# Last frequency group of tile 0 by sixteen combined matrices instead of through DRAM; two neighbouring pieces of work moved

## The chip, the cores and the metric

One core of one Trainium2 chip. The metric is the device time of one execution in microseconds. The kernel before took 700.67 us, the median of 3 runs (699.94 to 701.03).

## The reference

An adaLN block over 2048 tokens of width 512, batch 1. `mod = silu(c) @ w_mod` gives six rows of shifts, scales and gates.

```
h = layernorm(x) * (1 + ca) + sa
x = x + ga * S4(h)        # per channel: causal convolution of length 2048 by FFT, plus h * Dskip
h = layernorm(x) * (1 + cb) + sb
x = x + gb * (mish(h @ w1 + b1) @ w2)      # 512 -> 1792 -> 512
```

The convolution's kernel K(l) = Re sum_n C_n exp(dt A_n l) dt B_n has 128 complex terms per channel.

## The kernel before

**Convolution.** The 512 channels are four blocks b of 128. The transform over the 2048 tokens is done in two steps by matmuls, of length 32 and of length 64, with 32 frequencies r in the first. A block's frequencies go through in eight groups of four; v = 8b + s counts groups, so 24 to 31 belong to the last block. For a group, `s_ubu` (L575) and `s_ubk` (L591) take the input and the convolution's kernel through the step of length 64 with the matrices `mf` (128 x 32 x 128, group s reads slices 4s to 4s + 3), `s_ug` copies the first on ACT, `s_prod` (L597) multiplies the two spectra in four DVE operations, `s_t1` (L611) transposes the product on TensorE and copies it on ACT to `yt`, and `s_invb` (L618) applies the inverse of length 64 (`mi`), copies the result on ACT to `z`, and stores `z`, 256 KB, to DRAM (`zd`).

The inverse of length 32 sums over all 32 frequencies of a block, which lie on different partitions of what is needed, so it reads `zd` back as `zt`. Blocks 0 to 2 do it in `s_inva` with `inva_mm` (L669, one call for two token tiles, K = 64 matmuls with 32 columns of weights). A token tile j, 0 to 3, is 512 tokens. `inva_add` (L678) adds the result to x on DVE and stores x to DRAM (`x2d`).

**The last stage** is `drain` (L932), an order written out by hand. A loop over the last block's groups, i = 0 to 7, runs `s_prod`, a split of w1 (`w1_split`, L822: a rounded high part on ACT, the rest on DVE), the transforms for later groups, `s_t1` and `s_invb`. For the last block `zt3` is one tile of 128 partitions x 2 halves x 2048: `zt_rows(s)` (L952) loads group s, 32 rows of 8 KB, onto every fourth partition of half s // 4. `inva_half(h, js)` (L955) does the inverse of length 32 over one half, K = 128, for the token tiles js; PSUM adds the halves up. The loads of groups 0 to 4 are issued on SP at i = 3 to 7, behind that iteration's store of `z`; those of 5 and 6 on POOL; that of 7 on SP, and all later DMAs of certain kinds are pinned behind it (`pin["SP"]`).

Behind the loop: statistics of the layernorm for blocks 0 and 1, `inva_mm` for block 2 (two calls) with its adds, the first half of block 3 for all four token tiles, its second half for tile 0, `inva_add(b, 0)` and tile 0's statistics, the second half of tiles 1 to 3, `gate_row` (L489, four matmuls and ACT's copy `gbb`), then layernorm of tile 0: `ln_scales` (a row of small DVE operations), `ln_qs` (`xn`, two on DVE, two on ACT), `ln_tq` (transposes into `pln`), `ln_h` (`hh`, the MLP's input split in two).

**MLP.** Tile 0 goes through `mm1_plain(f)` for f = 0 to 13 with `load_w2(0, f)` (w2 is multiplied by the gate and split); `mm2(0, f - 2)` follows f by two. Tiles 1 to 3 run on a scheme with seven products. The splits of w1 number 5 to 7 and more serve f of 7 and up.

**Order.** TensorE, ACT and DVE run in the order of the program in `drain` and for f = 0 and 1 (`InOrder`, L123). SP's and POOL's order is chosen by the framework's planner, with program order as priority; tiles of a pool share buffers: `z` has three, `w1s`, `w2s` share three (tag `ws`), most PSUM results share six banks (tag `pb`).

Of the kernel before, what the change touches and what calls it, by code (L numbers as in the profile page):

```python
# [18 lines left out]
P = 128  # L19
# [33 lines left out]
def _constants():  # L53
    r = np.arange(32)
    s = np.arange(64)
    j = np.arange(64)
    i = np.arange(32)
    th = 2 * np.pi * ((j[None, :, None] * (4 * r[:, None, None] + 1 + 128 * s[None, None, :])) % 8192) / 8192.0
    mf = np.zeros((32, 2, 64, 2, 64))
    mf[:, 0, :, 0, :] = np.cos(th)  # L60
    mf[:, 1, :, 0, :] = np.sin(th)
    mf[:, 0, :, 1, :] = -np.sin(th)
    mf[:, 1, :, 1, :] = np.cos(th)
    mf = mf.reshape(32, P, P)
    psi = 2 * np.pi * ((i[:, None] * (4 * r[None, :] + 1)) % 128) / 128.0
    da = np.stack([np.cos(psi), -np.sin(psi)], axis=1)
    bdk = np.zeros((4, 32, 2, 4, 32))
    for t in range(4):
        bdk[t, :, :, t, :] = da
    da = da.transpose(0, 2, 1).reshape(32, 64)  # L70
    dj = np.zeros((8, 4, 4, 2, 4, 32))
    for j in range(4):
        dj[:, j, :, :, j, :] = da.T.reshape(2, 4, 8, 32).transpose(2, 1, 0, 3) / 2048.0
    ac = np.zeros((4, 32, 32, 32))
    mc = np.zeros((4, 32, 32, NCO))
    fac = np.concatenate([64 * 8 * np.arange(4), 64 * np.arange(8), 8 * np.arange(8), np.arange(8)])
    for d in range(32):
        ac[0:2, d, d, :] = np.arange(32)
        ac[2:4, d, d, :] = 1
        mc[0:2, d, d, :] = fac  # L80
        mc[2:4, d, d, :4] = 1
    z = np.exp(-2j * np.pi * (4 * np.arange(2048) + 1) / 8192)
    one = ((1 + 1j) / (1 - z)).reshape(64, 8, 4)
    one = np.stack([one.real, one.imag]).transpose(2, 0, 3, 1).reshape(4, 2, 512)
    su = np.zeros((4, 32, 2, 512))
    hl = np.zeros((P, 2))
    for e in range(3):
        m, x = np.frexp(one)
        part = np.ldexp(np.round(m * 256) / 256, x)
        one = one - part  # L90
        for n in range(3):
            su[:, 3 * n + e] = part
            hl[3 * n + e::32, :n] = -1
    f = np.float32
    return {
        "su": su.reshape(P, 1024).astype(f),
        "hl": hl.astype(f),
        "mf": np.ascontiguousarray(mf.transpose(1, 0, 2).reshape(P, 32 * P)).astype(f),
        "mi": np.ascontiguousarray(mf.transpose(2, 0, 1).reshape(P, 32, 2, 4, 4, 4).transpose(0, 1, 2, 4, 3, 5)
                                   .reshape(P, 32 * P)).astype(f),  # L100
        "bdk": np.ascontiguousarray(bdk.transpose(0, 1, 2, 4, 3)).reshape(P, 256).astype(f),
        "bdu": np.tile(da, (4, 1)).astype(f),
        "di": np.tile(da.T / 2048.0, (2, 1)).astype(f),
        "di4": dj.reshape(P, 256).astype(f),
        "ac": ac.reshape(P, 1024).astype(f),
        "mc": mc.reshape(P, 32 * NCO).astype(f),
        "sel": np.tile(np.concatenate([np.eye(32, P, 32 * k) for k in range(4)], axis=1), (4, 1)).astype(f),
        "ident": np.eye(P, dtype=f),
    }
# [9 lines left out]
def s4_block(ctx, tc, io, out):  # L119
    nc = tc.nc  # L120
# [60 lines left out]
    def view(src, offset, ap):  # L181
        return bass.AP(tensor=src.tensor, offset=src.offset + offset, ap=ap)
# [378 lines left out]
    def s_gl(v):  # L561
        b, s = divmod(v, 8)
        GU[v] = cv.tile([P, 512], F32, tag="gu", name=f"gu{v}", bufs=4).rearrange("p (r d) -> p r d", r=4)
        nc.sync.dma_start(GU[v], view(ud, (64 * b + 8 * s) * 64 * P, [[P, P], [P * P, 4], [1, P]]))
# [53 lines left out]
    def s_invb(v):  # L618
        b, s = divmod(v, 8)
        p = bank("pib")  # L620
        for r in range(4):
            T.matmul(p[:, P * r:P * r + P], mi[:, 4 * s + r, :], YT[v][:, r, :], start=True, stop=True)
        z = cv.tile([P, 4, P], F32, tag="us", name=f"z{v}", bufs=3)
        A.copy(z, p.rearrange("p (r d) -> p r d", r=4))
        nc.sync.dma_start(view(zd[b], 8 * s * 64 * P, [[P, P], [P * P, 4], [1, P]]), z)
# [41 lines left out]
    PIA = {}  # L667

    def inva_mm(b, j):  # L669
        for h in range(2):  # L670
            PIA[b, j + h] = bank("pia")
        for a in range(4):
            for h in range(2):
                r = slice(64 * h, 64 * h + 64)
                T.matmul(PIA[b, j + h][32 * a:32 * a + 32, :], di[r, :], ZT[b, j, a // 2 * 2][r, a % 2, :],
                         start=True, stop=True)
# [255 lines left out]
    def drain():  # L932
        b = NB - 1
        bulk[0] = nc.gpsimd
        tables("mish")
        for v in range(v0 + 2, v0 + 5):
            s_gl(v)
        s_kgen(vl)
        s_ks(vl)
        s_t1(v0 - 1)  # L940
        s_ubu(v0 + 1)
        s_ka(vl)
        s_ug(v0 + 1)
        s_tm(vl)
        s_invb(v0 - 1)
        s_ubk(v0)
        mlp_open()
        s_xp(v0 - 1)
        bulk[0] = nc.sync
        zt = big.tile([P, 2, 4, 512], F32, tag="gk", name="zt3")  # L950

        def zt_rows(s, queue):  # L952
            return queue.dma_start(zt[s % 4::4, s // 4], view(zd[b], 8 * s * 64 * P, [[16 * P, 32], [1, 2048]]))

        def inva_half(h, js):  # L955
            for j in js:
                for a in range(4):
                    T.matmul(PIA[b, j][32 * a:32 * a + 32, :], di4[:, h, j, :], zt[:, h, a, :],
                             start=(h == 0), stop=(h == 1), skip_group_check=True)

        def on_pool(f, *a):
            bulk[0] = nc.gpsimd
            f(*a)
            bulk[0] = nc.sync

        for v in range(v0, NG):
            i = v - v0
            s_prod(v)
            if i != 3 and i < 7:
                w1_split(i - i // 4)  # L970
            if i < 3:
                on_pool(w1_load, i + 3)
            if v < vl:
                s_ubk(v + 1)
            if i == 0:
                s_ubu(v + 2)
            s_t1(v)
            if v + 2 <= vl:
                if i:
                    s_ubu(v + 2)  # L980
                s_ug(v + 2)
            if v + 5 <= vl:
                s_gl(v + 5)
            s_invb(v)
            if i in (1, 2):
                s_zl(v0 - 6 + 2 * i)
            if i >= 3:
                zt_rows(i - 3, nc.sync)
        zt_rows(5, nc.gpsimd)
        zt_rows(6, nc.gpsimd)  # L990
        pin["SP"] = zt_rows(7, nc.sync).ins
        ln_stats(0, range(b - 1))
        inva_mm(b - 1, 0)
        inva_add(b - 1, 0)
        inva_mm(b - 1, 2)
        ln_stats(0, (b - 1,))
        for j in range(1, 4):
            inva_add(b - 1, j)
        p = psum.tile([P, 2, 512], F32, tag="pa", name="pia2", bufs=1)
        PIA.update({(b, 0): bank("pia"), (b, 1): bank("pia"), (b, 2): p[:, 0], (b, 3): p[:, 1]})  # L1000
        inva_half(0, range(4))
        inva_half(1, (0,))
        inva_add(b, 0)
        ln_stats(0, (b,))
        inva_half(1, range(1, 4))
        gate_row()
        ln_scales(0)
        xn = cv.tile([P, 4, NB, P], F32, tag="gk", name="xn", bufs=1)
        ln_qs(0, xn)
        for j in range(1, 4):  # L1010
            inva_add(b, j)
        for q in range(4):
            for c in range(NB):
                ln_tq(xn, q, c)
        ln_h()
# [187 lines left out]
    for f in range(FB):  # L1203
        if f == 2:
            pin["V"] = ordered["V"]
            del ordered["V"], ordered["A"]
        if f == FB - 1:
            ln_sums(1)
        mm1_plain(f)
        load_w2(0, f)  # L1210
        if f in (2, 3):
            w1_load(4 + f)
        if f in (4, 5):
            w1_split(2 + f)
        if f in (11, 12):
            ln_at(1, 2 * f - 22)
        if f >= 2:
            mm2(0, f - 2, first=(f == 2))
        if f in (11, 12):
            ln_at(1, 2 * f - 21)  # L1220
        if f >= 2:
            next(todo, None)
        if f == 7:
            ln_load(1)
        if f == 8:
            ln_stats(1, range(2))
        if f == 9:
            ln_stats(1, range(2, NB))
            ln_norm(1)
        if f == 10:  # L1230
            fin_load(0)
# [76 lines left out]
```

## Time and profile before

| what | value |
| --- | --- |
| median of 3 runs | 700.67 us |
| the profiled execution | 699.58 us, span 697.8 us |
| TensorE busy | 628.7 us, 90% of the span |
| DVE, ACT, POOL busy | 496.0, 373.5, 78.5 us |
| mean granted TensorE clock | 0.978 |
| the convolution's last stage, `drain` | ends with `hh`, from 385.19 us |

Times in the profile count from the span's start. PE is TensorE, DVE VectorE, ACT ScalarE, POOL GpSimd, SP the engine that issues most DMAs. An fp32 matmul is two instructions. Names are the program's tiles without their numbers: `pkb` and `pub` are the transforms of kernel and input, `pt` the transpose, `pib` the inverse of length 64, `pia` that of length 32, `pgb` the gate row, `pln` the transposes of the layernorm, `pr` and `pp` the MLP. All compute carries line L131, that of the ordering helper, so the names tell operations apart. A timeline row holds start, length, engine, line, operation, tiles, shape, count, and in brackets the idle time before it with what ended it. A row of the windows holds the stretch, its length, then busy time and count of PE, PEld, DVE, ACT and POOL, the granted clock, the DMA share and GB/s. A row of DMA issues ends with the median us from issue to landing.

### The profile page before, as it was taken

The page shows a single profiled execution, that of the slowest core. Times are in us where ns is not written, and L with a number is a line of the kernel's source. Part 1 is how long each engine was busy: PE and PEld are TensorE (multiplying, and loading weights), DVE is VectorE, ACT ScalarE, POOL GpSimd, SP SyncE. Part 2 cuts the span into 40 slices and gives each one's busy share as a digit, 9 for nine tenths or more (in the row PEclk, how much of TensorE's full clock was granted, in tenths as well). Part 3 has the DMA queues.
Part 4 walks back from the last instruction along what each step waited for, and adds up shares of the span by engine and source line. Part 5 has one row for each costly group of instructions (what it writes and reads, how often), then busy time and mean ns, then how long its engine had stood idle before and what let it go on. Part 6 is the DMA issues. An engine that isn't in the chain of part 4 may idle for free.

```text
span 697.8 us, 15159 instructions
## 1 busy us (share of the span) xinstructions
PE 628.7 (90%) x6077; PEld 512.0 (73%) x6106; DVE 496.0 (71%) x1005; ACT 373.5 (54%) x618; POOL 78.5 (11%) x161
## 2 busy tenths in 40 slices
PE   0566787899999999999987999999999999999997
PEld 0353355677878877888773788888898888998996
DVE  6989986898899988997575799577327733553333
ACT  3465479566886677666561565443436334443231
POOL 1000340060204220000100000000011000010000
PEclk9968989999999999999999999999999999999999
DMA  9928789674328752654687789557334652264232
GB/s 235 220 113 271 182 191 221 190 196 127 77 62 196 196 140 62 167 163 143 181 253 220 233 268 319 183 162 225 112 91 118 193 173 91 92 193 140 91 91 60
DMA packets 107399, 115.89 MB, mean 166 GB/s; under 512 B 12737, under 2 KB 84801, under 8 KB 106433
## 3 DMA queue, kind: packets, MB, share of 16 engines
q1 hardware_dynamic: 93712, 86.34, 43.9%
q0 software_dynamic: 13232, 28.06, 14.4%
q8 instruction: 48, 0.79, 0.5%
q10 hardware_dynamic: 384, 0.52, 0.3%
q14 instruction: 23, 0.18, 0.1%
HBM read 80.28 MB, written 32.51 MB: 162 GB/s over the span
## 4 chain that ended last, share of the span: by engine, by line
PE 71%; DVE 14%; DMA 6%; ACT 5%; issue 2%; SPq 2%; ACTq 0%; DVEq 0%
PE pr L131 29%; PE pp L131 10%; PE pub L131 6%; PE pang L131 6%; PE pkb L131 4%; PE pib L131 4%; PE pkg L131 4%; PE pka L131 4%; DVE ec L131 3%; DVE raw L131 2%; PE pt L131 2%; DMA xt<-x2d 2%; DMA ud<-us 1%; DMA cT<-in_c 1%; DVE bst L131 1%
## 5 line engine op out<-in xcount | busy, mean ns | idle before, releaser
L131 DVE TENSOR_TENSOR ec<-ec,m 128x1024 f32<-128x1024 f32 (+1 forms) x96 | 97.2, 1040 | 13.0 <-ACT ec L131 12.7
L131 ACT ACTIVATE ec<-pang 128x1024 f32<-128x1024 f32 x64 | 65.1, 1034 | 53.9 <-PE pang L131 53.9
L131 PE MATMUL pr<-hh,w 128*128 128x256 f32 (+1 forms) x420 | 78.2, 327 | 0.5 <-ACT hh L131 0.5
L131 PEld LDWEIGHTS pr<-hh,w 128*128 128x128 f32 x420 | 66.5, 188 | 12.7 <-ACT hh L131 1.9
L131 DVE TENSOR_TENSOR mh<-x,pr 128x256 f32<-128x256 f32 x63 | 26.4, 418 | 65.2 <-PE pr L131 64.9
L131 PE MATMUL pp<-w,mah 128*128 128x512 f32 x224 | 70.5, 396 | 0.0
L131 PE MATMUL pr<-w,mah 128*128 128x512 f32 x224 | 70.2, 394 | 0.2 <-DVE w L131 0.2
L131 ACT ACTIVATE mh<-mh,b 128x256 f32<-128x256 f32 x63 | 32.1, 510 | 55.0 <-DVE mh L131 54.7
L131 DVE TENSOR_TENSOR m<-co 128x1024 f32<-128x1024 f32 (+1 forms) x64 | 59.6, 950 | 1.7 <-ACT co L131 1.4
L131 ACT ACTIVATE mh<-pr,b 128x256 f32<-128x256 f32 (+1 forms) x35 | 19.5, 559 | 65.0 <-PE pr L131 65.0
L1033 POOL DMA_DIRECT2D w<-w2d x42 | 22.2, 529 | 282.8 <-PE pp L131 272.1
L131 DVE TENSOR_TENSOR mal<-mh,mah 128x512 fp32r<-128x512 f32 x56 | 38.5, 688 | 21.7 <-ACT mah L131 21.6
L131 PE MATMUL pr<-w,mal 128*128 128x512 f32 x112 | 43.9, 392 | 0.0
L131 PE MATMUL pp<-w,mal 128*128 128x512 f32 x112 | 43.9, 392 | 0.0
L131 PE MATMUL pka<-bdk,ks 128*64 128x128 f32 x512 | 35.9, 284 | 6.9 <-ACT ks L131 6.9
L131 PEld LDWEIGHTS pp<-w,mah 128*128 128x128 f32 x224 | 38.3, 189 | 4.9
L131 DVE TENSOR_TENSOR x<-x,pr 128x256 f32<-128x256 f32 x42 | 17.5, 418 | 33.5 <-PE pr L131 33.5
L131 PE MATMUL pang<-ac,s 128*128 128x256 f32 x128 | 30.0, 318 | 12.2 <-ACT ec L131 12.2
L350 POOL DMA_DIRECT2D s<-pk x48 | 23.8, 504 | 147.9 <-ACT us L131 77.1
L131 PE MATMUL pang<-nac,s 128*128 128x256 f32 x128 | 39.8, 395 | 0.0
L131 PEld LDWEIGHTS pr<-hh,wt 128*128 128x128 f32 x252 | 35.5, 190 | 5.5 <-DVE mh L131 2.2
L131 PEld LDWEIGHTS pkg<-ec 128*32 128x32 f32 x2048 | 33.0, 111 | 8.8 <-ACT us L131 3.2
(153 smaller groups left out, 1351.1 us busy)
## 6 DMA issues: line engine op xcount, KB each, us to landing
w<-w2d POOLq DMA_DIRECT2D x42, 512.0 KB, 3.6
ud<-us SPq DMA_DIRECT2D x64, 128.0 KB, 3.0
gu<-ud SPq DMA_DIRECT2D x32, 256.0 KB, 3.6
zd<-z SPq DMA_DIRECT2D x32, 256.0 KB, 3.6
zt<-zd SPq DMA_DIRECT2D x30, 256.0 KB, 5.1
w2d<-w SPq DMA_DIRECT2D x14, 512.0 KB, 4.1
wm<-in_w_mod SPq DMA_DIRECT2D x24, 256.0 KB, 3.6
xf<-x2d SPq DMA_DIRECT2D x16, 256.0 KB, 4.7
```

The source lines that it names most:

```text
L131: ins = f(*a, **kw)
L350: nc.gpsimd.dma_start(S3[b, i][q, :], pk[32 * i:32 * i + 32, 8 + k, :])
L1033: nc.gpsimd.dma_start(t, w2d[f])
```

## The change

1. For group 31 and token tile 0 alone, the inverses of length 64 and 32 are multiplied together beforehand into sixteen 128 x 128 matrices, `dx` (four frequencies times four tokens of a quad; 1 MB, a new constant). `direct()` applies them to `yt` of group 31 and adds into tile 0's PSUM bank. Tile 0's second half then contracts 96 rows, groups 4 to 6. Group 7's rows are still loaded, for tiles 1 to 3.
2. `dx` is loaded on POOL at i = 3 into slices 0 to 15 of `mf`, whose groups are through by then.
3. `zt_rows(s)` fills 32 neighbouring partitions; the constant `di4` is reordered to match. All eight loads are on SP, each one iteration earlier (group 0 at i = 2); groups 6 and 7 follow the loop.
4. Block 2's two calls of `inva_mm` move from behind the loop to i = 6 and 7, between the transpose and `s_invb`.
5. The first half of tiles 1 to 3 moves behind tile 0's second half.
6. `w1_split(5)` moves from i = 6 into the MLP, behind `load_w2(0, 0)`.

```diff
-    dj = np.zeros((8, 4, 4, 2, 4, 32))
+    dj = np.zeros((4, 8, 4, 2, 4, 32))
     for j in range(4):
-        dj[:, j, :, :, j, :] = da.T.reshape(2, 4, 8, 32).transpose(2, 1, 0, 3) / 2048.0
+        dj[:, :, j, :, j, :] = da.T.reshape(2, 4, 8, 32).transpose(1, 2, 0, 3) / 2048.0
+    dx = np.einsum("rcajq,rci->qrjai", mf.reshape(32, 2, 4, 4, 4, P)[28:, :, :, 0], da.T.reshape(32, 2, 32)[28:] / 2048.0)
...
+        "dx": dx.reshape(P, 16 * P).astype(f),
...
         def zt_rows(s, queue):
-            return queue.dma_start(zt[s % 4::4, s // 4], view(zd[b], 8 * s * 64 * P, [[16 * P, 32], [1, 2048]]))
+            return queue.dma_start(zt[32 * (s % 4):32 * (s % 4) + 32, s // 4], view(zd[b], 8 * s * 64 * P, [[16 * P, 32], [1, 2048]]))
 
-        def inva_half(h, js):
+        def inva_half(h, js, rows=P):
             for j in js:
                 for a in range(4):
-                    T.matmul(PIA[b, j][32 * a:32 * a + 32, :], di4[:, h, j, :], zt[:, h, a, :],
+                    T.matmul(PIA[b, j][32 * a:32 * a + 32, :], di4[:rows, h, j, :], zt[:rows, h, a, :],
                              start=(h == 0), stop=(h == 1), skip_group_check=True)
 
+        def direct():
+            for r in range(4):
+                for j in range(4):
+                    T.matmul(PIA[b, 0][:, P * j:P * j + P], mf[:, 4 * r + j, :], YT[vl][:, r, :], start=False, stop=False,
+                             skip_group_check=True)
...
-            if i != 3 and i < 7:
+            if i != 3 and i < 6:
                 w1_split(i - i // 4)
...
+            if i >= 6:
+                inva_mm(b - 1, 2 * i - 12)
             s_invb(v)
+            if i == 3:
+                nc.gpsimd.dma_start(mf[:, 0:16], io["dx"].rearrange("p (n m) -> p n m", n=16))
             if i in (1, 2):
                 s_zl(v0 - 6 + 2 * i)
-            if i >= 3:
-                zt_rows(i - 3, nc.sync)
-        zt_rows(5, nc.gpsimd)
-        zt_rows(6, nc.gpsimd)
+            if i >= 2:
+                zt_rows(i - 2, nc.sync)
+        zt_rows(6, nc.sync)
         pin["SP"] = zt_rows(7, nc.sync).ins
         ln_stats(0, range(b - 1))
-        inva_mm(b - 1, 0)
         inva_add(b - 1, 0)
-        inva_mm(b - 1, 2)
...
-        inva_half(0, range(4))
-        inva_half(1, (0,))
+        inva_half(0, (0,))
+        direct()
+        inva_half(1, (0,), 96)
         inva_add(b, 0)
         ln_stats(0, (b,))
+        inva_half(0, range(1, 4))
         inva_half(1, range(1, 4))
         gate_row()
...
         load_w2(0, f)
+        if f == 0:
+            w1_split(5)
         if f in (2, 3):
```

## The prediction

> **What bounds the kernel now.** I read the chain that ended last first, from 360 us on, because the change lies between the last frequency groups of the convolution and the first matmul of the MLP. Columns: start, length, what.
>
> ```profile
> 362.20 0.85 ACT w L131
> ...
> 363.07 1.09 DVE w L131
> 364.17 1.27 DVE q L131 x2
> ...
> 365.46 0.77 DVE ug L131 x2
> ...
> 366.36 0.64 PE pt L131 x4
> ...
> 367.08 0.59 ACT yt L131
> ...
> 367.72 2.09 PE pib L131 x8
> ...
> 369.83 0.60 ACT z L131
> ...
> 370.44 2.61 DMA zd<-z
> ...
> 373.07 4.11 DMA zt<-zd
> ...
> 377.32 1.10 PE pia L131 x8
> ...
> 385.19 0.79 ACT hh L131
> ```
>
> The stretch is serial. The sixth split of w1 (ACT then DVE `w`) holds the product of group 31 (`q`, `ug`); the transpose, its copy `yt`, the inverse `pib` and the copy `z` follow; then z goes to DRAM and back, 2.61 + 4.11 = 6.72 us in which tile 0 waits. From `hh` on the chain is mostly TensorE's, so what `hh` gains, the span should gain.
>
> The TensorE timeline shows what can fill the gap:
>
> ```profile
> 361.42 1.06 PE L131 MATMUL pkb<-mf,gk 128*128 128x128 f32 x8
> 362.31 0.60 PE L131 MATMUL pt<-ident,ug 128*128 128x128 f32 x4
> 363.64 1.16 PE L131 MATMUL pib<-yt,mi 128*128 128x128 f32 x8 [0.73 <-ACT yt L131]
> ...
> 369.72 6.07 PE L131 MATMUL pia<-zt,di 64*32 64x512 f32 x64
> 377.32 3.64 PE L131 MATMUL pia<-zt,di 128*32 128x512 f32 x32 [1.52 <-DMA zt<-zd]
> 380.89 1.16 PE L131 MATMUL pgb<-ident,modp 128*128 128x128 f32 x8
> ```
>
> An inverse of eight instructions takes 1.16 us here; the last, at 367.72, took 2.09, because the idle time before it had halved the granted clock (the column before the last two is the clock):
>
> ```profile
> 368.00:370.00 2.00, 2.00 (x16) 1.72 (x24) 0.00 (x0) 0.17 (x1) 0.53 (x1) 0.50 0.33 118
> ```
>
> The row at 369.72 holds block 2's inverse (32 instructions) and the first half of block 3's (32). The second half, 32 instructions for four j's from 377.32 until the gate row starts at 380.89, gives 3.57/4 = 0.89 us for one j of one half.
>
> **The change, part by part.** *The split that leaves i = 6.* The product of group 31 then waits only for `pkb`, which ends at 362.48. With 0.1 of issue it starts near 362.57 instead of 364.17, 1.6 us earlier, and ends 2.06 later (364.17 to 366.23), at 364.63. With the chain's 0.13 and 0.64 the transpose ends at 365.41.
>
> *Block 2's inverse moved into i = 6 and 7.* In the steady loop one such call of 16 instructions stands in this row:
>
> ```profile
> 231.07 1.09 PE L131 MATMUL pia<-zt,di 64*32 64x512 f32 x16
> 232.09 1.16 PE L131 MATMUL pib<-yt,mi 128*128 128x128 f32 x8
> ```
>
> It holds TensorE 1.02 us. The first call goes from 362.75 to 363.77 in the 0.73 us of waiting for `yt`, and delays group 30's inverse from 363.64 to 363.77, 0.13 us. The second follows the transpose, from 365.25 to 366.27, while ACT copies `z` of group 30 and `yt` of group 31 (0.59 each, the second ending near 366.17). Group 31's inverse can start at 366.27. Without the idle stretches ahead of it I price it at 1.16, not 2.09: it ends at 367.43, `z` at 368.05, and the store goes at 368.07 instead of 370.44, 2.37 us earlier. The four results of block 2 now hold banks of PSUM through this; with the six there are I count no wait, and the adds that free them follow the last product on DVE.
>
> *The sixteen direct matrices.* 16 matmuls of 128 columns are 32 instructions; at 0.89 us for eight (`pkb`, 361.42 to 362.31) they cost 3.6 us of TensorE that was not there before. TensorE is free of the inverse at 367.27; one j of the first half takes until 368.16, the sixteen until 371.8. Their weights are one megabyte, loaded through POOL at i = 3, behind this load:
>
> ```profile
> 350.22 0.54 POOL L817 DMA_DIRECT2D w1s<-in_B_w  x1 [4.25 <-DVE q L131]
> ```
>
> ```profile
> w1s<-in_B_w POOLq DMA_DIRECT2D x1, 448.0 KB, 6.2
> ```
>
> ```profile
> mf<-in_mf SPq DMA_DIRECT2D x1, 2048.0 KB, 8.6
> ```
>
> Issued at 350.8, it takes between 8.6/2 = 4.3 us and 6.2 x 1024/448 = 14.2 us: landed by 365.0, before 368.16. For the sixteen I cost it at nothing. But the queues are full there (the last two columns are the DMA share and GB/s):
>
> ```profile
> 355.00:360.00 5.00, 4.74 (x36) 3.83 (x35) 4.12 (x6) 3.58 (x6) 0.00 (x0) 1.00 1.06 312
> 360.00:362.00 2.00, 2.00 (x21) 2.00 (x20) 1.97 (x5) 1.07 (x2) 0.00 (x0) 1.00 0.63 202
> 362.00:364.00 2.00, 1.27 (x12) 1.03 (x11) 1.07 (x2) 1.59 (x3) 0.00 (x0) 1.00 0.44 132
> 364.00:366.00 2.00, 0.80 (x8) 0.61 (x6) 1.97 (x5) 0.59 (x1) 0.52 (x1) 1.00 0.51 139
> ```
>
> One megabyte at 312 GB/s is 3.4 us of backlog, and the idle shares from 360 to 366 add up to 2 x (0.37 + 0.56 + 0.49) = 2.8 us. So it is nearly taken in by 366; for the rest I put 0.2 us on group 6's rows (ends: 0 and 0.6). If it isn't, the stores land late, and `z`, which has three buffers, waits for the store three groups back.
>
> *The row loads.* All eight now issue on SP, behind the stores in program order. Before, group 4's sat behind the last store, at 370.44, with group 7's behind it (the merged row's other one):
>
> ```profile
> 370.90 2.62 SPq L953 DMA_DIRECT2D zt<-zd  x2
> ```
>
> So I place the loads of groups 5 and 6 behind the store at 368.07, 0.46 and some 0.5 us on: 368.5 and 369.0, and with the backlog 369.2. Group 7's waits there for the store's landing, 368.07 + 2.63 = 370.7; block 2's stores of x, pinned behind it, issue some 2.4 us earlier than before and nobody on the path waits for them. Tile 0 now needs group 6's rows last. Landing times of such loads in this stage, first group 6's on POOL, then the one behind the store, at 370.90:
>
> ```profile
> zt<-zd POOLq DMA_DIRECT2D x1, 256.0 KB, 2.9
> ```
>
> ```profile
> zt<-zd SPq DMA_DIRECT2D x1, 256.0 KB, 4.0
> ```
>
> I take 4.0, the row with the same neighbour: landed at 373.2, matmul at 373.3. The quick end is 369.0 + 2.9 = 371.9, and then the sixteen matrices' end and this come together.
>
> *What is late next.* Call the start of the second half's first j t. Before, t = 377.32, and behind it stood three j's (2.7 us), the gate row, ACT's copy `gbb`, ACT's two `xn`. Behind it now stand six j's, since the first half of j = 1 to 3 has moved behind tile 0's.
>
> ```profile
> 382.08 0.59 ACT L131 COPY gbb<-pgb 128x512 f32<-128x512 f32 x1 [11.66 <-PE pgb L131]
> 382.97 1.52 ACT L131 ACTIVATE xn<-xt,nm,rst 128x512 f32<-128x512 f32 x2 [0.30 <-DVE nm L131]
> 385.19 2.79 ACT L131 ACTIVATE hh<-pln,modp 128x512 fp32r<-128x512 f32 x4 [0.70 <-PE pln L131]
> ```
>
> Before, `xn` waited for DVE's `nm`, 382.97 - 377.32 = 5.65 behind t. Now it waits for `gbb`: 7 x 0.893 + 1.16 + 0.03 + 0.59 + 0.02 = 8.05 behind t. So 2.4 us are given back: this is the wait that takes the place of the one removed. With 385.19 - 382.97 = 2.22 more, `hh` starts at t + 10.27, and the change breaks even at t = 374.92. With t = 373.3, `hh` starts at 383.57: **1.6 us earlier**.
>
> *The split moved to f = 0.* It costs 0.85 us of ACT and 1.09 of DVE (the chain's `w`).
>
> ```profile
> 398.61 0.69 DVE L131 TENSOR_TENSOR w<-w2s,w 128x512 fp32r<-128x512 f32 x1
> ...
> 401.13 0.62 PE L131 MATMUL pr<-w,mah 128*128 128x512 f32 x2
> ```
>
> Behind it in order are f = 1's mish, splits and w2: DVE's last of these ends at 399.3, and TensorE asks for it at 401.13, 1.8 us later. The two pieces, 1.94 us in a row, just use that up if nothing of them falls into idle time; I take nothing (ends: 0 and 0.3). The third load of w2 may have to wait for the buffer; its use comes after TensorE's next two matmul groups.
>
> **Sum.** 377.32 - 373.3 = 4.0 us earlier for tile 0's last input, less 2.4 behind it: 1.6 us. The profiled execution took 699.58 (span 697.8), so 698.0 for it; the median of the runs shown is 700.67, 1.1 above it, and from there I predict **699.1 us**. What a measurement of this kernel can tell from no change is about 0.2%, 1.4 us.
>
> **Rivals.** *The sixteen matrices are the bound* (0.16): group 6's rows land within 2.9 us, t = 371.8, `hh` 3.1 us earlier, 697.6. For it: the row of 2.9. Against: that load had no store and no other rows just ahead.
>
> *The new row layout is slow* (0.21). The loads now fill 32 neighbouring partitions instead of every fourth. The first stage loads `xr` in just that shape, 32 partitions by 8 KB, and then `mf` over all 128:
>
> ```profile
> 14.00:18.00 4.00, 0.00 (x0) 0.00 (x0) 3.69 (x13) 1.81 (x3) 0.00 (x0) 1.00 1.04 225
> ...
> 34.00:36.00 2.00, 0.00 (x0) 0.00 (x0) 1.90 (x6) 1.98 (x2) 0.00 (x0) 0.50 1.12 408
> ```
>
> Queues full in both, 225 against 408 GB/s: 256 KB take 1.17 instead of 0.64 us. Groups 5 and 6 behind the store would land 1.0 later, with group 4's tail up to 1.6: t = 374.3 to 374.9, gain 0 to 0.6, 700.4. Against it: part of the `xr` stage is shared with POOL's loads. [...]
>
> *The change doesn't do what it says* (0.09): the 96-row matmuls still wait for group 7's rows, if the order is kept for the whole tile. Then t = 370.7 + 4.11 + 0.14 = 374.9, no gain, 700.6; with slow rows 1.2 us slower. Against it: the 32 instructions of the first half ran before 375.8, while rows of the other half landed until 377.18, so parts of that tile are told apart at least by half.
>
> *Slower* (0.08): the megabyte goes into the half of `mf` that the loop has done with. If the order is kept for `mf` as one, the load waits for the last reader ahead of it, `pub` in i = 3, and the next reader, `pkb` behind the inverse, waits for its landing:
>
> ```profile
> 351.57 1.41 PE pub L131 x9
> 352.98 0.91 PE pib L131 x8
> ```
>
> Issued at 353.0, in 8 us (between the 4.3 and 14.2 above), it lands at 361.0, and `pkb` stands from 353.9 till then: 7.1 us less the 1.6 gained, 5.5 slower, 706.2. It decides as soon as one reader of slices 16 to 31 waits. Against it is again what `zt` shows.
>
> **How the numbers follow.** Forecast 0.46 (t from 372.4 to 374.2, 697.8 to 700.0). Faster: the matrices and the part of the forecast with t under 373.5, for which I put 0.39 of its 0.46: 0.55 together. Same: the rest of the forecast, 0.07, the slow layout and two thirds of the whole-tile wait: 0.34. Slower: the rest of that and `mf`, 0.11. The range goes from the matrices' case, 697.3 with the scatter of the runs, to 701.4, which takes in the slow layout and most of the whole-tile wait; it leaves out about 0.12.
>
> **What would show it.** Right: no `w` between the last two products; the last inverse near 1.2 us at full clock; the last store near 368; `pia` of K = 96 before group 7's rows land; `gbb` ending just ahead of `xn`. If `xn` waits for `nm` instead, the step of 2.4 us is wrong. If `pia` starts over 4.4 us after group 6's issue, the landing is. A PE gap near 401 would be the split; one in `pkb` near 354 the megabyte.

## The result and the profile after

In runs taken side by side the changed kernel took 701.38 us (median of 20) and the kernel before 700.88 (median of 20): a ratio of 1.0007, with a 95% interval of 0.9991 to 1.0023. That is no difference that can be measured: 0.5 us more, between 0.6 less and 1.6 more. The forecast was 1.6 us less.

The profiled execution took 700.8 us, span 699.0, granted clock 0.980. A span alone says little here. Group 30's product starts at 361.20 in this trace and at 360.00 in that of before, but at 184 us, long before anything that was changed, the trace is 1.2 us behind already; over the fourteen executions profiled in this study the product lies anywhere from 359.01 to 363.85. So I compare lengths inside the stage, counted from the start of group 30's product on DVE: to **t**, where TensorE starts block 3's second half for tile 0, and to `hh`, where the MLP starts.

| | before | after | predicted change | measured change |
| --- | --- | --- | --- | --- |
| group 30's product to group 31's | 4.08 us | 2.58 us | -1.6 | -1.50 |
| to the last store's issue | 10.44 | 8.26 | -2.37 | -2.18 |
| to t | 17.32 | 14.32 | -4.0 | -3.00 |
| t to `hh` | 7.87 | 9.93 | +2.40 | +2.06 |
| to `hh` (the stage) | 25.19 | 24.25 | -1.6 | -0.94 |
| `hh` to the end of the span | 312.61 | 313.57 | 0 | +0.96 |

The chain that ended last in the changed kernel, to be read beside that of before (start, length, what):

```profile
367.72 1.10 PE pib L133 x8
...
368.85 0.60 ACT z L133
...
369.46 0.36 SPq L627
...
369.91 0.45 SPq L955
...
370.42 4.96 DMA zt<-zd
...
375.52 6.22 PE pia L133 x56
381.74 1.10 PE pgb L133 x8
...
382.86 0.03 ACT gbb L133
...
383.34 0.82 ACT xn L133
...
385.45 0.79 ACT hh L133
```

The turn through DRAM for group 31, 2.61 + 4.11 us, is gone from the path. In its place stands the load of group 30's rows, 4.96 us, and then a row that was not there: `pia` x56, all of what is left of the four tiles, with the gate row and its copy `gbb` behind it. Before, the chain's `pia` was 8 instructions long and DVE's statistics came next. TensorE's timeline and ACT's say the same; the brackets hold the wait and its end:

```profile
367.65 1.16 PE L133 MATMUL pib<-yt,mi 128*128 128x128 f32 x8
368.74 1.06 PE L133 MATMUL pia<-zt,di 128*32 128x512 f32 x8
369.73 3.84 PE L133 MATMUL pia<-yt,mf 128*128 128x128 f32 x32
375.52 6.22 PE L133 MATMUL pia<-zt,di 96*32 96x512 f32 x56 [1.95 <-DMA zt<-zd]
```

```profile
382.86 0.59 ACT L133 COPY gbb<-pgb 128x512 f32<-128x512 f32 x1 [13.43 <-PE pgb L133]
383.34 1.52 ACT L133 ACTIVATE xn<-xt,nm,rst 128x512 f32<-128x512 f32 x2
```

The sixteen direct matrices (32 instructions) are done 1.95 us before the rows land. `xn` starts 383.34 - 375.52 = 7.82 us behind t with no wait of its own, straight after `gbb`; `nm`, for which it waited before, had ended at 381.15. The queues, in the windows of the changed kernel (the last two columns are the DMA share and GB/s), stay full until 366, where before they had emptied to shares of 0.63, 0.44 and 0.51:

```profile
355.00:360.00 5.00, 4.74 (x40) 4.18 (x39) 3.11 (x5) 3.93 (x6) 0.00 (x0) 1.00 1.03 369
360.00:362.00 2.00, 2.00 (x16) 1.61 (x16) 1.81 (x3) 0.77 (x3) 0.00 (x0) 1.00 1.03 288
362.00:364.00 2.00, 2.00 (x20) 1.88 (x18) 1.52 (x4) 1.25 (x2) 0.00 (x0) 1.00 1.09 358
364.00:366.00 2.00, 2.00 (x26) 1.12 (x24) 1.97 (x5) 0.59 (x1) 0.00 (x0) 1.00 1.08 332
```

### The profile page after: what moved, and what is told of

It is laid out like the page before. It is cut to its first block, busy times and chain, and to the rows that moved or that the text cites. A ratio compares the mean times of both kernels' runs of the same rounds, so it can differ in the third digit from the quotient of the medians.

```text
span 699.0 us, 15258 instructions
## 1 busy us (share of the span) xinstructions
PE 633.9 (91%) x6138; PEld 515.0 (74%) x6138; DVE 496.4 (71%) x1005; ACT 373.8 (53%) x618; POOL 78.3 (11%) x160
## 4 chain that ended last, share of the span: by engine, by line
PE 68%; DVE 15%; DMA 7%; ACT 5%; issue 3%; SPq 1%; ACTq 0%; DVEq 0%
PE pr L133 25%; PE pp L133 9%; PE pub L133 6%; PE pang L133 6%; PE pkb L133 4%; PE pkg L133 4%; PE pib L133 4%; PE pka L133 3%; DVE ec L133 2%; DMA xt<-x2d 2%; DVE raw L133 2%; PE pt L133 2%; PE pia L133 2%; ACT ec L133 2%; DMA wm<-in_w_mod 1%
## 5 line engine op out<-in xcount | busy, mean ns | idle before, releaser
L133 PE MATMUL pang<-rnd,oneb 128*128 128x512 bf16 x128 | 41.9, 410 | 0.0
L352 POOL DMA_DIRECT2D s<-pk x48 | 25.2, 551 | 149.3 <-ACT us L133 77.1
```

Source lines behind the costliest of these rows:

```text
L133: ins = f(*a, **kw)
L352: nc.gpsimd.dma_start(S3[b, i][q, :], pk[32 * i:32 * i + 32, 8 + k, :])
```

## The theories

So 3.0 us were won at t and 2.06 given back behind it. **The order theory**: the first halves of tiles 1 to 3 and the gate row, now queued behind t on TensorE, hold `xn`, and with another order the 2 us come back. **The queue theory**: the megabyte of combined matrices is what makes stores and rows late, and so t. **The layout theory**: it is the rows' 32 neighbouring partitions. Against all three: the direct matrices are worth nothing, and what gain there is comes from the pieces moved. Twelve runs tell them apart. The table has them all; a ratio is to the kernel before on the same chip, t and `hh` are from the profiled execution.

| run | ratio (95% interval) | product of 30 to t | t to `hh` | stage |
| --- | --- | --- | --- | --- |
| before | 1 | 17.32 us | 7.87 | 25.19 |
| changed kernel | 1.0007 (0.9991 to 1.0023) | 14.32 | 9.93 | 24.25 |
| e1, first halves ahead | 0.9963 (0.9942 to 0.9984) | 17.27 | 7.88 | 25.15 |
| e2 and e11, gate row ahead | 0.9959 (0.9939 to 0.9979) | 13.64; 14.14 | 7.88; 7.89 | 21.52; 22.03 |
| e3, before with the new row layout | one run, 701.58 us | 16.47 | 9.05 | 25.52 |
| e4, rows 5 and 6 on POOL | one run, 703.55 us | 14.25 | 11.63 | 25.88 |
| e5, split back | 1.0017 (0.9997 to 1.0037) | 15.83 | 9.93 | 25.77 |
| e6, e1 without the direct matrices | 1.0018 (1.0000 to 1.0036) | 15.75 | 10.19 | 25.94 |
| e7, e1 without the megabyte | 0.9970 (0.9954 to 0.9986) | 14.86 | 7.88 | 22.75 |
| e9, e1 with the megabyte early | 0.9972 (0.9954 to 0.9990) | 14.87 | 7.88 | 22.75 |
| e10, e6 with the old row layout | 1.0003 (0.9980 to 1.0027) | 14.66 | 8.86 | 23.52 |
| e12, e11 with the megabyte early | 0.9967 (0.9945 to 0.9989) | 14.12 | 7.88 | 21.99 |
| e13, e11 with the inverse back | 0.9985 (0.9963 to 1.0006) | 14.85 | 7.89 | 22.74 |

## What holds xn: the order behind t

**e1, all first halves ahead of the direct matrices.**

```diff
-        inva_half(0, (0,))
+        inva_half(0, range(4))
         direct()
...
-        inva_half(0, range(1, 4))
         inva_half(1, range(1, 4))
         gate_row()
```

> The changed kernel with one line's order undone: the first half of all four token tiles stands ahead of the sixteen matrices again. The stage is measured from the start of group 30's product to the start of hh: 25.19 us before (360.00 to 385.19), 24.25 changed (361.20 to 385.45). Theory (the order gives 2.4 us back): three j's at 0.89 us move into TensorE's wait for group 6's rows; its work then ends near 368.74 + 3.57 + 3.84 = 376.1, so t moves from 375.5 to 376.1, but only the gate row and three j's stand behind it, xn waits for nm at t + 5.65 and hh starts at t + 7.87 = 384.0: stage 22.8, 1.5 us shorter than changed. Rival (the order is not what holds xn): the stage gets longer by 0.6, 24.9. In all runs a median of about 699.4 for the theory and 701 for the rival.

Measured: ratio 0.9963 (0.9942 to 0.9984), faster than before. `xn` waits for `nm` again:

```profile
383.26 0.58 ACT L133 COPY gbb<-pgb 128x512 f32<-128x512 f32 x1 [12.85 <-PE pgb L133]
384.17 1.53 ACT L133 ACTIVATE xn<-xt,nm,rst 128x512 f32<-128x512 f32 x2 [0.32 <-DVE nm L133]
```

t to `hh` is 7.88 us, that of before. Its profiled execution shows no gain in the stage for another reason: the stores were late in it, and ACT's copy of `z` for group 30 stood 2.68 us for a store, which put t where it was before. The median of the twelve times is lower all the same; e7 and e9, which have the same instructions from there on, reach t 14.86 us behind the product.

**e2 and e11, the gate's row alone moved ahead.** The first halves of tiles 1 to 3 stay behind t.

```diff
         direct()
+        gate_row()
         inva_half(1, (0,), 96)
...
         inva_half(1, range(1, 4))
-        gate_row()
```

> The changed kernel with the gate's row alone moved ahead of block 3's last half, right behind the direct matrices; the first halves of the other three tiles stay behind it. By the theory that the gate's copy behind the other tiles' halves holds xn, gbb's copy is done before nm, add to hh is 6.75 us as before the change (8.81 in the changed kernel), and the stage 15.4 + 6.75 = 22.2 us where the queues are as in the changed kernel's profile. The rival, that the halves themselves are what is late (PE's order behind t costs the same whatever holds xn), leaves add to hh at 8 us or more.

> The changed kernel with the gate's row alone moved ahead of block 3's last half, as in the single look at it (694.4 us, with 2.2 us of that already there at group 30's product, which scatters from run to run). By the stage alone, 21.52 us from group 30's product to hh against 25.19 before the change, the median is 3.7 us under before: 697.2, ratio 0.9948. If the look was a lucky one and what is late is the landing of the rows, the stage is 23.5 to 25 us as in the changed kernel and the ratio is 0.998 or more. The run with all first halves ahead (ratio 0.9963) lies between.

Measured: one execution of 694.4 us in e2, then over twelve executions in e11 a median of 697.44 against 701.09, ratio 0.9959 (0.9939 to 0.9979). The stages, 21.52 and 22.03 us, say 3.2 to 3.7 us; the median says 3.65, by the ratio 2.9. TensorE and ACT in e11:

```profile
371.08 3.84 PE L133 MATMUL pia<-yt,mf 128*128 128x128 f32 x32
374.75 1.06 PE L133 MATMUL pgb<-ident,modp 128*128 128x128 f32 x8
375.74 6.22 PE L133 MATMUL pia<-zt,di 96*32 96x512 f32 x56
381.98 1.94 PE L133 MATMUL pln<-ident,xn 128*128 128x128 f32 x16
```

```profile
375.84 0.59 ACT L133 COPY gbb<-pgb 128x512 f32<-128x512 f32 x1 [6.02 <-PE pgb L133]
381.41 1.52 ACT L133 ACTIVATE xn<-xt,nm,rst 128x512 f32<-128x512 f32 x2 [4.98 <-DVE nm L133]
```

The same 56 `pia` stand behind t, 6.22 us long, and cost nothing: `xn` waits for DVE's `nm` and starts 5.67 us behind t, and `pln` follows the 56 at once. What cost 2 us was only that eight instructions and a copy, which need nothing of tile 0's sum, were queued last. The order theory holds; the rival in e2's expectation, that the halves themselves are late, falls. e2 and e11 are the same program; in e2 TensorE waited 0.17 us for rows ahead of tile 0's first half, in e11 0.88, and the stages differ by 0.51.

## What makes the rows late

**e3, the kernel before with the new row layout and nothing else** (the constant `di4` reordered, as in the change).

```diff
-            return queue.dma_start(zt[s % 4::4, s // 4], view(zd[b], 8 * s * 64 * P, [[16 * P, 32], [1, 2048]]))
+            return queue.dma_start(zt[32 * (s % 4):32 * (s % 4) + 32, s // 4], view(zd[b], 8 * s * 64 * P, [[16 * P, 32], [1, 2048]]))
```

> The kernel before with one part of the change alone: each row load fills 32 neighbouring partitions, the constant reordered to match; queues and order as before. Landing of the loads before: 2.9 (group 6, POOL), 4.0 (group 4, behind the last store), 4.1 us (group 7). Theory (the layout is slow): each of the last ones lands 0.5 to 1.0 us later, group 7's in 4.6 to 5.1, and the stage grows from 25.19 to 25.7 to 26.2. Rival (the layout is innocent and the changed kernel's 4.96 us is crowding behind the store): 2.9, 4.0 and 4.1 as before, within 0.2, and a stage of 25.2.

Measured: the loads of groups 0 to 3 and 5 take 0.1 to 0.6 us longer (group 5's on POOL 3.45 against 2.98, group 3's 4.23 against 3.67); group 4's takes 5.08 against 3.98, and group 6's 5.22 against 2.87, but it was issued right behind the last store here and ahead of it before. Group 7's, for which tile 0 waits, takes 4.29 against 4.11. The two loads on POOL, as a row of DMA issues in e3:

```profile
zt<-zd POOLq DMA_DIRECT2D x2, 256.0 KB, 4.3
```

Before it was 2.9. The stage is 25.52 us against 25.19, one execution each, and that difference says little of the layout: the last inverse ran at full clock here, 1.16 us in place of 2.09, which takes 0.9 us off, and behind TensorE's wait of 2.14 us the clock was halved (0.50 from 380 to 382), so that t to `hh` took 9.05 in place of 7.87.

**e10 against e6: the layout without the direct matrices.** e6 is e1 without `direct()`, without the load of `dx`, and with all 128 rows in the second half; e10 is e6 with the layout and the constant of before.

```diff
-            if i == 3:
-                nc.gpsimd.dma_start(mf[:, 0:16], io["dx"].rearrange("p (n m) -> p n m", n=16))
...
-        direct()
-        inva_half(1, (0,), 96)
+        inva_half(1, (0,))
```

> The kernel of the run with all first halves ahead, with the sixteen direct matrices and their megabyte left out: block 3 of tile 0 takes all 128 rows of its second half again, so it waits for group 7's rows too; w1's sixth split and block 2's inverse stay where the change put them. This asks what the direct matrices themselves are worth. Theory A (the direct path takes the wait for group 7's rows away): block 3's last half starts when group 7's rows land. Group 31's store is issued 5.2 to 5.3 us behind group 31's product at the earliest with the moved inverse (369.46 - 363.79 = 5.67 in the changed kernel, 370.44 - 363.81 = 6.63 in the run with all first halves ahead), lands 2.6 to 3.5 us later, and the rows take 4.1 to 4.5: from group 30's product to the add 2.58 + 5.67 + 3.0 + 4.3 + 1.1 = about 16.7 with quiet queues, against 15.4 of the changed kernel; since xn waits for nm again (add to hh 6.75), the stage from group 30's product to hh comes to 23.4, and the time to about 698.7, nothing lost against the run with all first halves ahead. Theory B (the megabyte of the direct matrices is what crowds the queues): stores of groups 27 to 30 land in 6.2, 6.6, 4.3 and 2.3 as before the change, not in 8.4 to 11.7, and the stage is shorter than the 25.15 of the run with all first halves ahead by over 1 us. Theory C (the direct path is worth what it says and the megabyte costs nothing): the stores land as late as with it, and the stage is longer by over 1 us.

> The run without the direct matrices, with the rows laid out as before the change (every fourth partition instead of 32 neighbours); nothing else differs from it, and no megabyte is loaded in either. If the row layout is what makes the rows land late, the loads of groups 0 to 2 take 6.7, 4.5 and 3.1 us as before the change, not 10.2, 9.7 and 6.9, group 6's take 2.9 to 4.1 and not 4.5, and the stage falls from 25.94 by 0.5 to 1.5 us. If the rows are late because each load is issued one group earlier, ahead of the store that it waits for, they take 9 us or more in the old layout too, and the stage stays within 0.5 us of 25.9.

The last store and the rows behind it, from the chains of e6 and then of e10:

```profile
370.33 3.86 DMA zd<-z
...
374.21 3.49 DMA zt<-zd
...
377.83 6.47 PE pia L133 x32
```

```profile
368.61 2.35 DMA zd<-z
...
370.98 3.90 DMA zt<-zd
...
375.01 1.97 PE pia L133 x8
```

DMA by DMA, the rows of groups 0 to 2 land in 10.23, 9.72 and 6.91 us in e6 and in 7.63, 7.34 and 5.01 in e10, those of groups 5 and 6 in 4.36 and 4.50 against 3.04 and 3.17. So group 6's load takes about 1.3 us longer in the new layout, and the store beside it too (3.86 against 2.35). These are single executions, but over all ten kernels that issue that load on SP in the new layout it takes 3.90 (e7) to 5.85 us (e1), so e10's 3.17 lies below them all. Of the 2.42 us between the two stages 1.09 lie ahead of t; the rest lies behind it, where e6's clock was halved for longer (0.50 in the windows from 378 to 382, in e10 in the one from 376 to 378). The first three rows are still later in e10 than the 6.71, 4.45 and 3.05 of before, in the same layout; they are issued one group earlier, as the second theory of e10's expectation has it. That this is the reason is argued, since e10 has other pieces of the change as well. Both theories hold in part. The medians do not tell the layouts apart (1.0018 and 1.0003, intervals that overlap). For such a load 4.50 us against 3.17 is 1.4 times as long, where the prediction's two rates, 408 and 225 GB/s, give 1.8; why the layout makes a difference no run shows.

**e7 and e9: the megabyte.** e7 is e1 without the load of `dx`. e9 is e1 with `dx` in a tile of its own, loaded before the loop.

```diff
+        dxt = MW["wt"].tile([P, 16, P], F32, tag="dxt", name="dxt", bufs=1)
+        nc.gpsimd.dma_start(dxt, io["dx"].rearrange("p (n m) -> p n m", n=16))
...
-            if i == 3:
-                nc.gpsimd.dma_start(mf[:, 0:16], io["dx"].rearrange("p (n m) -> p n m", n=16))
```

> The kernel of the run with all first halves ahead without the load of the megabyte of combined matrices: the sixteen matmuls still run, but on what the buffer held from block 2's own matrices, so that the last group of tile 0 is computed wrongly; its time is read for the queues alone. If the megabyte is what delays the stores and rows, those of groups 27 to 29 land in 6.2, 6.6 and 4.3 us as before the change (8.4, 8.8 and 6.5 in the changed kernel, 10.6, 11.7 and 8.7 in the run with all first halves ahead), group 6's rows take 4.0 to 4.4, group 30's store is issued by 5.3 us behind group 31's product, the add of block 3 comes 14.8 to 15.2 us behind group 30's product and hh 21.6 to 22 us: 698.5 to 697.5 by the sums of before. If the row layout or the earlier rows are the cause, the stores land as late as with the megabyte and the stage keeps 24 to 25 us.

> The kernel of the run with all first halves ahead with the combined matrices in a tile of their own, loaded at the start of the drain instead of at its fourth group; the computation is whole. If the megabyte in the middle of the stores is the cost, the landings are those of the kernel without the load (6.2, 6.6, 4.3 for groups 27 to 29, group 6's rows 4.0 to 4.4), the stage from group 30's product to hh takes 21.6 to 22.5 us instead of 25.19 before, and the time is 2.5 to 3.5 us under before: 697.3 to 698.3, ratio about 0.9955. If it is not, the time is that of the run with all first halves ahead, 0.9963, with a stage of 24 to 25 us. If the earlier megabyte delays what else is loaded there (x of the last block, w1), the drain starts later instead, and group 30's product with it, by up to the 2.8 us that a megabyte takes at 370 GB/s.

Measured: the store of group 26 is back at 6.14 us in e7 (8.44 in the changed kernel), but those of 27 and 28 stay at 8.36 and 6.14, and the rows of groups 0 to 2 take 9.03, 8.59 and 6.56 with no megabyte at all. One execution says little: e6, the same program up to there, has 8.43 us for group 26. Over all kernels but before and e3, whose rows are issued later, group 27's store lands in 8.80 to 11.68 us with the megabyte in the middle and in 6.80 to 9.71 without it there (e6, e7, e9, e10, e12), so it does delay the stores beside it. The ratios, 0.9963 with the megabyte in the middle, 0.9970 without it and 0.9972 with it early, do not differ. In e7 and e9 TensorE's own work sets t (7.33 and 7.34 us of it stand between the last inverse and t, with no wait), so neither can show a gain there; e12 below can, and shows none. The queue theory falls: the megabyte delays the DMAs next to it and not the end. (e9's product of group 30 is late, at 363.85 us; in e12, with the same early load, it starts at 359.27, so the load is not what delays it.)

In e7 TensorE runs from the last inverse to the gate row without a wait:

```profile
367.83 1.16 PE L133 MATMUL pib<-yt,mi 128*128 128x128 f32 x8
368.92 3.64 PE L133 MATMUL pia<-zt,di 128*32 128x512 f32 x32
372.49 3.84 PE L133 MATMUL pia<-yt,mf 128*128 128x128 f32 x32
376.25 3.64 PE L133 MATMUL pia<-zt,di 96*32 96x512 f32 x32
```

That is the rival "the sixteen matrices are the bound", made true by e1's order: 7.33 us of work stands ahead of t, and the rows of group 6, landed at 375.58, wait for it.

**e12, both mends at once** (e11 with `dx` in a tile of its own).

> Both mends at once: the gate's row ahead of block 3's last half, and the combined matrices in a tile of their own, loaded at the start of the drain. If the megabyte in the middle of the stores still costs, the stores of groups 26 to 28 land in 7.1 to 8.7 us instead of 9.4 to 9.5, group 6's rows start up to 0.5 us earlier, and the stage is 20.8 to 21.4 us: ratio 0.994. If the megabyte costs nothing once the order is mended, the time is that of the gate's row alone, 0.9948 by its stage. The earlier megabyte may also be paid ahead of the stage: group 30's product at 363.85 in the run with the tile of its own against 359.0 to 361.2 elsewhere; if that is no scatter, the ratio is 0.998 or more with a short stage.

Measured: 0.9967 (0.9945 to 0.9989), stage 21.99 us. The stores do land earlier (8.24, 6.80, 6.07, 3.70 us for groups 26 to 29), and neither the stage nor the median is better than e11's.

**e4, rows of groups 5 and 6 on POOL**, as before the change.

```diff
-            if i >= 2:
+            if 2 <= i < 7:
                 zt_rows(i - 2, nc.sync)
-        zt_rows(6, nc.sync)
+        zt_rows(5, nc.gpsimd)
+        zt_rows(6, nc.gpsimd)
```

> The changed kernel with the loads of groups 5 and 6 on POOL behind the loop again, as before; the layout stays. Group 6's load then issues when group 30's store has landed, not behind group 31's store: near 369.9 instead of 370.4 in the changed kernel's times. Theory (layout): it takes 3.5 to 4 us where the old layout took 2.9, landing 373.4 to 373.9, and t is set by TensorE, 373.6 to 374.0: the stage is 22.4 to 22.8. Rival (crowding behind the store): 2.9 us as before, landed 372.8, t = 373.6 by TensorE alone, stage 22.3. If group 6's load still takes 5 us, neither: the queues as a whole are full.

Measured: the two loads take 5.83 and 5.45 us from POOL, and t is no earlier (14.25 us). The last store took 5.37 us to land, and group 7's rows left at 376.19. Neither theory had that. What made it so stays open. The two loads landed at 375.48 and 376.72 us and the store at 376.18, while between 374 and 376 the DMA engines as a whole were almost idle; the share, the last column but one, is 0.08, 1.3 of the sixteen engines it is counted over:

```profile
374.00:376.00 2.00, 0.95 (x9) 0.76 (x7) 0.00 (x0) 0.00 (x0) 0.00 (x0) 1.00 0.08 21
```

So it is not the traffic as a whole that was short at that point. t to `hh`, 11.63 us against 9.93 in the changed kernel, is the clock's: TensorE ran the 56 instructions without a wait among them, at a granted clock of 0.50 from 378.01 to 381.42 (windows in the last section), in 7.92 us where the changed kernel needs 6.22.

```profile
376.81 7.92 PE L133 MATMUL pia<-zt,di 96*32 96x512 f32 x56 [1.86 <-issue]
```

## What the single pieces are worth

**The direct matrices: e6.** Without them, with the moves kept, the kernel is no faster than before (1.0018, 1.0000 to 1.0036); with them and e1's order it is 0.9963. By these medians theory C of e6's expectation holds, and theory A falls. The matrices do what they are for, t no longer waits for group 31's rows (14.86 us behind the product in e7, 15.75 in e6), and one thing more. With them gone TensorE has nothing to do while it waits; in e6 the second half starts behind 4.42 us of waiting, and the windows show the granted clock (third from the right):

```profile
374.00:376.00 2.00, 0.00 (x0) 0.00 (x0) 0.00 (x0) 0.00 (x0) 0.00 (x0) 1.00 0.39 71
376.00:378.00 2.00, 0.17 (x4) 0.20 (x8) 0.00 (x0) 0.00 (x0) 0.00 (x0) 0.69 0.98 334
378.00:380.00 2.00, 2.00 (x12) 0.49 (x11) 0.18 (x1) 0.00 (x0) 0.00 (x0) 0.50 1.06 342
```

Its 32 `pia` take 6.47 us where e7's take 3.64, and t to `hh` 10.19 in place of 7.88. So in these two executions the halved clock costs 2.3 of the 3.2 us between the stages; none of the theories had it. e10, without the matrices and with the old row layout, reaches t 14.66 us behind the product, no later than e7 with them, and loses 0.98 us behind t at half clock (0.50 from 376 to 378). What the matrices would be worth with the old layout is not known: no run has both, and the contraction of 96 rows needs the new one, since in the old one group 7's rows lie between the others'.

**The split: e5**, the changed kernel with `w1_split(5)` at i = 6 again.

> The changed kernel with the sixth split of w1 back at i = 6. Two questions. In the stage: the product of group 31 waits for the split again, 1.6 us, and with it the last store, group 6's load and t: the stage grows from 24.25 to about 25.8. From hh to the end of the span: 312.6 us before, 313.6 changed. Theory (the moved split reorders DVE, ACT and SP in the MLP and costs 1 us there): 312.6 again, since the orders of DVE and ACT are those of before. Rival (scatter between runs): anything from 312.4 to 313.6 without regard to it. In the median the two cancel for the theory: 701.3; 702 for the rival.

Measured: ratio 1.0017 (0.9997 to 1.0037), stage 25.77 us, where 25.8 was expected. Group 31's product is 4.08 us behind group 30's again, as before the change. One row of it shows the wait for `z`'s three buffers that the prediction named as the price of a backlog; it is ACT's copy of `z` for group 30:

```profile
368.40 0.58 ACT L133 COPY z<-pib 128x512 f32<-128x512 f32 x1 [1.56 <-DMA zd<-z]
```

**Block 2's inverse: e13**, e11 with the two calls behind the loop again.

```diff
-            if i >= 6:
-                inva_mm(b - 1, 2 * i - 12)
...
+        inva_mm(b - 1, 0)
         inva_add(b - 1, 0)
+        inva_mm(b - 1, 2)
```

> The run with the gate's row ahead, with block 2's inverse back behind the last group, where it stood before the change. Theory A (with the direct matrices, block 3 waits for group 30's rows and not for group 31's, and the inverse's first call, 1.02 us, stands ahead of group 30's own last inverse): undoing the move sends group 30's store 0.5 to 1 us earlier and group 31's later, and the stage is 20.6 to 21.5 us, no longer than with it. Theory B (the prediction: the move takes the two calls out of the stretch behind the last group, so that the direct matrices are done before the rows land): the calls, 2.04 us together, come ahead of the direct matrices again, PE's 1.95 us of waiting for the rows is used up, and the stage is 21.5 to 22.5 us; group 31's store leaves 6.4 us behind its product, not 5.7, and the rows of group 31, which tiles 1 to 3 need, land some 1 us later.

Measured: 0.9985 (0.9963 to 1.0006), stage 22.74 us against 21.52 and 22.03. TensorE in e13:

```profile
367.13 1.16 PE L133 MATMUL pib<-yt,mi 128*128 128x128 f32 x8 [0.73 <-ACT yt L133]
368.22 2.94 PE L133 MATMUL pia<-zt,di 64*32 64x512 f32 x40
371.09 3.84 PE L133 MATMUL pia<-yt,mf 128*128 128x128 f32 x32
374.76 1.06 PE L133 MATMUL pgb<-ident,modp 128*128 128x128 f32 x8
375.75 6.22 PE L133 MATMUL pia<-zt,di 96*32 96x512 f32 x56
```

The inverse's 32 instructions are back in the row at 368.22, TensorE is busy until t, and t is the end of its work. Theory B holds: the move is worth about 0.7 to 1.2 us of the stage, because it clears the stretch behind the last group (the medians, 0.9985 against 0.9959, point the same way, with intervals that overlap). Little of theory A is left: without the move group 30's store leaves 0.2 us earlier and not 0.5 to 1, and group 31's does not leave later but earlier too, 5.46 us behind its product in place of 5.67. The 6.4 us that theory B gave it is wrong as well; the inverse takes 1.16 us here too.

## Why the prediction came out as it did

The median, 701.38 us, lies 0.02 us inside the upper end of the range that was given, 701.4; the point, 699.1, was 2.3 us too low, and "faster" had been given more chance (0.55) than "same" (0.34). The range reached that far for two rivals, the slow layout and the whole-tile wait, and not for the forecast's own sum, so it is luck that the result lies in it as far as that sum goes. In the stage the sum was off at two terms: at the rows it promised 1.0 us too much, and behind t it gave back 0.3 us too much.

**The split that leaves i = 6** was right: 1.50 us against 1.6, and e5 gives it back whole.

**Block 2's inverse moved** was right in its sum, the last store 2.18 us earlier against 2.37, and wrong in its cause. The 0.93 us of the last inverse, 2.09 to 1.16, was not won by the move: in e13 it takes 1.16 without it (there the split's move has taken the longest of the waits away), and in e3 as well, which has the waits of before (0.73, 1.57 and 0.73 us) and the same order. What I took for a rule was one throw of the clock. The move pays elsewhere, on the direct matrices' path.

**The sixteen direct matrices** were right in size, 3.84 us in the row against 3.6, and done before the rows. Their load went ahead of w1's and not behind it, at 349.73, and landed in 8.83 us, in time. Wrong was that the megabyte's backlog is taken in by 366: the queues were full until then. Of the causes, the row layout is shown (e10) and the earlier issue argued; the megabyte delays stores and makes no difference to the end that the runs can tell (e12).

**The row loads** are the term that was mis-sized. The landing was put at 4.0 us from the row with the same neighbour; it took 4.96, and from the last store's issue to t 6.06 us passed against 5.2. Counted from the changed kernel's later start (1.20 us), t = 374.3 and not 373.3. That is the lower edge of the rival "the new row layout is slow", t from 374.3 to 374.9 and a gain of 0 to 0.6 us, which was given a chance of 0.21; e10 against e6 shows the delay that it names, with 1.3 us for group 6's load where the rival had 1.0 to 1.6.

**What is late next** was right: `gbb` takes the place of `nm`, 7.82 us behind t against 8.05, 2.06 us given back against 2.40. e11 shows that this was the larger loss of the two, and that it was a matter of eight instructions' place.

**The split moved to f = 0** costs nothing in the first 60 us of the MLP. The hundredth matmul instruction behind `hh` starts 24.65 us behind it in before and 24.67 in the changed kernel. The 0.96 us that its profiled MLP is longer come later, from 60 us behind `hh` on, in waits for DVE among others. TensorE's waits between 440 and 490 us in the changed kernel (total, times, longest; before has 1.0 us in two waits there, the longest 0.9):

```profile
PE pr L133 <- DVE mh L133: 1.2, 2, 0.9
PE pp L133 <- DVE xf L133: 0.3, 1, 0.3
```

e1 and e11 have the split in the same place and MLPs of 311.96 and 311.82 us; over all kernels it is 311.8 to 314.9. So the move does not cost that by itself, and what makes one execution's MLP longer stays open. Open too is why the changed kernel's median shows 0.5 us more while its profiled stage is 0.94 us shorter: the interval of the ratio ends at 0.6 us less.

Of the other rivals, the whole-tile wait and the load of `mf` kept as one are out: `pia` of K = 96 started at 375.52, before group 7's rows landed (372.95 + 3.70 = 376.65), and `pkb` ran on behind the load.

## What to carry to other kernels

When a wait is taken away, list what is queued behind it in order on each engine and who needs it: a small piece that does not depend on the late input, here the gate row, belongs ahead of the wait. A piece of work that fills a wait can be worth more than its place, where TensorE would come out of the wait at half clock, as it did in e6 (0.50 behind 4.42 us). And where stages scatter by 5 us ahead of the change, measure from the last event before it, and trust the medians of a dozen executions over one span.

## What the runs showed of the hardware

**The clock after a wait.** Single waits of TensorE of 1.37 (e1), 1.52 (before), 1.95 (after) and 1.97 us (e5) left the granted clock at 1.00 for the matmuls behind them. Waits of 1.86 (e4), 2.14 (e3), 3.48 (e10) and 4.42 us (e6) were followed by 0.50. So around 1.9 us the length of the wait does not decide. In e3 and e4 the halving came after TensorE had been let go, at 378.22 and 376.81. First e3, then e4 in stretches cut at the clock's changes, which shows half clock for 3.41 us:

```profile
376.00:378.00 2.00, 0.08 (x4) 0.00 (x0) 0.00 (x0) 0.00 (x0) 0.00 (x0) 1.00 0.85 303
378.00:380.00 2.00, 1.78 (x16) 0.69 (x20) 0.66 (x1) 0.00 (x0) 0.00 (x0) 0.79 1.02 373
380.00:382.00 2.00, 2.00 (x16) 0.64 (x12) 1.86 (x12) 0.00 (x0) 0.00 (x0) 0.50 0.71 224
```

```profile
374.60:378.01 3.41, 1.55 (x16) 0.66 (x18) 0.08 (x1) 0.00 (x0) 0.00 (x0) 1.00 0.26 55
378.01:381.42 3.41, 3.41 (x20) 1.09 (x16) 3.14 (x16) 0.00 (x0) 0.00 (x0) 0.50 1.01 360
381.42:384.84 3.42, 3.42 (x33) 1.14 (x26) 2.41 (x10) 0.00 (x0) 0.00 (x0) 1.00 0.67 213
```

Three short waits, 0.73, 1.56 and 0.73 us within 5 us, were followed by 0.50 in the kernel before (368 to 370); 0.73, 1.57 and 0.73 us in e3 by 1.00 (368 to 372). So nearly equal waits end in either clock, and what decides between them no run shows.

**Row loads that overlap.** The same 256 KB took 3.17 us in one layout and 4.50 in the other with the rest of the program equal (e10, e6; 3.90 to 5.85 over the other kernels with the second layout on SP), and up to 12.09 us where stores, rows and the megabyte were under way at once (e1, group 0).
